# Loads and filler at the start of a gated attention and gMLP kernel: split weight loads, another queue for the gate row, fewer filler matmuls

## Chip, cores and metric

The kernel runs on one core of one Trainium2 chip. The metric is the device time of one execution in microseconds (us); the median of several runs counts.

## What is computed

All arrays are bfloat16. x has 2048 rows of 512. Two mixers read the same x and are blended by a gate per row:

```python
g = sigmoid((x * gate_w).sum(-1, keepdims=True))
# A: linear attention, 32 heads of 16, with a learned feature map
q, k, v = split(x @ wqkv)                  # wqkv is 512 x 1536
phi(t) = concat(softmax(t @ w_phi), softmax(-(t @ w_phi)))
kv = sum_s phi(k)_s v_s ;  z = sum_s phi(k)_s
a = ((phi(q) @ kv) / (phi(q) . z + 1e-6)) @ wo
# B: gMLP, F = 1376, halves of 688
z = gelu(x @ w_in)                         # w_in is 512 x 1376
z1 = z[:, :688] ;  z2 = layernorm(z[:, 688:])
b = (z1 * (w_sp @ z2 + b_sp[:, None])) @ w_out      # w_sp is 2048 x 2048
out = g * a + (1 - g) * b
```

## The kernel before

Rows of x are handled in 16 tiles of 128 (index tt), the inner dimension of 512 in 4 blocks of 128 (index dt). The first stage computes z2 and z1 for all tiles: each tile needs 4 blocks times 2 column halves (j = 0, 1) of 344 columns, one matmul each (z_one, L195), with a transposed tile of x (xT) as weights and a block of w_in as moving data. The second half of w_in (for z2) is in the tile w_z2 and the first half (for z1) in w_z1. w_z2 has one column more, index 688, that holds gate_w, so that the matmul with j = 1 is 345 wide and gives the gate's logit on the side. That column is written by gate_T: gate_w is loaded as 4 rows of 128 (gaterow), transposed by a matmul with an identity (L294), and copied into w_z2 by VectorE (L295).

The order on TensorE and ScalarE is written out by hand (manual_schedule); VectorE and GpSimd are ordered by the tile framework. The head of the order is z2_first_two, which does tiles 0 and 1 together while their data arrive. It holds:

- warm_up(n, w): n filler matmuls of width w on constants, into a bank that is overwritten later (L226);
- x_T(i, d0, d1, ...): transposes of x tile i from the tile xs on TensorE (L284), copied to xT by VectorE (L290) or ScalarE (L287);
- one(tt, dt, j): one z_one matmul for tile tt, block dt, half j.

Then come z2 of tiles 2 and 3, z1 of tiles 0 to 3, and z2 and z1 of tiles 4 to 15 in groups of four, with the folding of w_phi into the query and key weights in between (wphi_fold, fold). After that come keys, values and the spatial product, then queries, attention and the output product.

Loads are issued from three queues, each in program order: SyncE (SP), ScalarE (ACT) and GpSimd (POOL). At the start ACT issues w_z2 blocks 0 and 1, the gate row and w_z2 block 3. SP issues xs tile 0, xs tile 1, w_z2 block 2, xs tiles 2 and 3 in one, then w_z1 in two loads, the transposing loads of x tiles 4 to 15 (L135, L137), w_phi (L140), the transposing load of the query and key weights (wqkT, L141), wv (L142) and the transposing loads of w_sp (wspT, L147). GpSimd issues the row of b_sp (L118) between its memsets. The framework gives the loads of SP and ACT together eight completion counters in turn, so that a load waits until the one eight places before it has landed. In the kernel before the first w_z1 load (L132) is the ninth, and waits for w_z2 block 0.

Of the kernel before, what the change touches and what calls it, by code (L numbers as in the profile page):

```python
# [14 lines left out]
P = 128  # L15
S = 2048
D = 512
H = 32
DH = 16
F = 1376  # L20
FH = 688
HF = FH // 2
NT = S // P
NDT = D // P
# [11 lines left out]
def kernel(  # L36
# [14 lines left out]
    nc = tc.nc  # L51
# [11 lines left out]
    w_z1 = early.tile([P, NDT, FH], BF16, name="w_z1")  # L63
    w_z2 = early.tile([P, NDT, WP], BF16, name="w_z2")
    wv_sb = kvw.tile([P, NDT, D], BF16, name="wv_sb")
# [29 lines left out]
    gaterow = early.tile([P, P], BF16, name="gaterow")  # L95
# [3 lines left out]
    w_in_v = B_w_in.rearrange("(dt p) f -> p dt f", p=P)  # L99
# [7 lines left out]
        out=ramp[:, 0, :], data0=ones32[:, :], data1=zeros[:, :], initial=0.0,  # L107
# [4 lines left out]
    for q in range(4):  # L112
        qs = slice(32 * q, 32 * q + 32)
        nc.vector.tensor_tensor(
            out=ident[qs, qs], in0=ramp[qs, 0, :], in1=ramp[qs, 1, :], op=ALU.is_equal)
    nc.gpsimd.memset(brow[:], 0.0)
    nc.gpsimd.memset(wphiE[:], 0.0)
    nc.gpsimd.dma_start(out=brow[0:NT, :], in_=B_b_sp.rearrange("(t p) -> t p", p=P))  # L118
    def load_z2w(eng, dt):
        eng.dma_start(out=w_z2[:, dt, 0:FH], in_=w_in_v[:, dt, FH:F])  # L120

    nc.sync.dma_start(out=xs[:, 0, :], in_=x2[0:P, :])
    load_z2w(nc.scalar, 0)
    nc.sync.dma_start(out=xs[:, 1, :], in_=x2[P:2 * P, :])
    load_z2w(nc.scalar, 1)
    load_z2w(nc.sync, 2)
    nc.scalar.dma_start(out=gaterow[0:NDT, :], in_=gate_w.rearrange("(dt p) -> dt p", p=P))
    load_z2w(nc.scalar, 3)
    nc.sync.dma_start(
        out=xs[:, 2:4, :], in_=x2[2 * P:4 * P, :].rearrange("(i p) d -> p i d", p=P))  # L130
    for h in range(2):
        nc.sync.dma_start(  # L132
            out=w_z1[:, 2 * h:2 * h + 2, :], in_=w_in_v[:, 2 * h:2 * h + 2, 0:FH])
    for i in range(4, 8):
        nc.sync.dma_start_transpose(out=xT[:, :, i * P:(i + 1) * P], in_=x2[i * P:(i + 1) * P, :])  # L135
    for q in range(2, NCH):
        nc.sync.dma_start_transpose(  # L137
            out=xT[:, :, q * CH:(q + 1) * CH], in_=x2[q * CH:(q + 1) * CH, :]
        )
    nc.sync.dma_start(out=wphiE[0:DH, :, :], in_=A_w_phi.rearrange("h e f -> e h f"))  # L140
    nc.sync.dma_start_transpose(out=wqkT[:, :, :], in_=A_wqkv[:, 0:2 * D])  # L141
    nc.sync.dma_start(  # L142
        out=wv_sb[:, :, :],
        in_=A_wqkv[:, 2 * D:3 * D].rearrange("(dt p) n -> p dt n", p=P),
    )
    for q in range(NCH):
        nc.sync.dma_start_transpose(  # L147
            out=wspT[:, :, q * CH:(q + 1) * CH], in_=B_w_sp[q * CH:(q + 1) * CH, :]
# [4 lines left out]
        out=eexp[:, :], in_=eexp[:, :], pattern=[[0, 8], [-1, 16]],  # L153
# [4 lines left out]
        out=mask_bd[:], in_=mask_bd[:], pattern=[[-16, 8], [0, 16]],  # L158
# [3 lines left out]
        out=mask_bd[:], in_=mask_bd[:], pattern=[[16, 8], [0, 16]],  # L162
# [4 lines left out]
        out=mask4[:], in_=mask4[:], pattern=[[-32, NG]],  # L167
# [3 lines left out]
        out=mask4[:], in_=mask4[:], pattern=[[32, NG]],  # L171
# [3 lines left out]
        out=mask64[:, :, :], in_=mask4[:, :, None].to_broadcast([P, NG, DH]))  # L175
# [7 lines left out]
    def next_turn(kind, n):  # L183
        turn[kind] += 1
        return f"{kind}{(turn[kind] - 1) % n}"

    def zp_tile():
        return psA.tile([P, 2, CH], FP32, name="zp", tag=next_turn("zp", 3))

    def pq_tile(shape, dtype=FP32):  # L190
        return psF.tile(shape, dtype, name="pq", tag=next_turn("pq", 2))

    def z_one(zp, tt, wt, w, dt, j):
        n = HF if j == 0 else w - HF
        nc.tensor.matmul(  # L195
            zp[:, j, 0:n], lhsT=xT[:, dt, tt * P:(tt + 1) * P],
            rhs=wt[:, dt, j * HF:j * HF + n],
            start=(dt == 0), stop=(dt == NDT - 1),
        )
# [8 lines left out]
    def z2_out(tt, zp):  # L208
        z2v = z2all[:, tt, :].rearrange("p (j n) -> p j n", j=2)
        nc.scalar.activation(out=z2v, in_=zp[:, :, 0:HF], func=AF.Gelu_apprx_tanh)  # L210
        nc.vector.tensor_copy(out=glog[:, tt:tt + 1], in_=zp[:, 1, HF:HF + 1])
        for j in range(2):
            nc.vector.bn_stats(out=bn6[:, tt, j, :], in_=z2v[:, j, :])  # L213
        nc.vector.bn_aggr(out=mv[:, tt, :], in_=bn6[:, tt, :, :].rearrange("p j s -> p (j s)"))
# [4 lines left out]
    def z2_first_two():  # L219
        zps = [zp_tile() for _ in range(2)]  # L220
        tp1 = psA.tile([P, 2, P], BF16, name="tp1", tag=next_turn("zp", 3))
        turn["zp"] -= 1

        def warm_up(n, w=CH):
            for _ in range(n):
                nc.tensor.matmul(  # L226
                    zps[0][:, 1, 0:w], lhsT=nc.const_aps.tensor(1.0, [P, P], BF16),
                    rhs=nc.const_aps.tensor(1.0, [P, w], BF16), start=True, stop=True)

        def one(tt, dt, j):  # L230
            z_one(zps[tt], tt, w_z2, FH + 1, dt, j)

        warm_up(6)
        warm_up(5, P)
        x_T(0, 0, 1, pq_tile([P, 1, P], BF16)[:, :, :])
        x_T(0, 1, NDT, pq_tile([P, 3, P], BF16)[:, :, :], on_act=True)
        warm_up(3, P)
        one(0, 0, 0)
        x_T(1, 0, 2, tp1[:, :, :])
        x_T(1, 2, NDT, pq_tile([P, 2, P], BF16)[:, :, :], on_act=True)  # L240
        one(0, 1, 0)
        warm_up(2, P)
        one(1, 0, 0)
        one(1, 1, 0)
        gate_T()
        one(0, 2, 0)
        one(1, 2, 0)
        for dt in range(2):
            one(0, dt, 1)
            one(1, dt, 1)  # L250
        one(0, 2, 1)
        one(1, 2, 1)
        x_T(2, 0, NDT, pq_tile([P, NDT, P], BF16)[:, :, :])
        one(0, 3, 0)
        one(0, 3, 1)
        z2_out(0, zps[0])
        one(1, 3, 0)
        one(1, 3, 1)
        z2_out(1, zps[1])
        x_T(3, 0, NDT, pq_tile([P, NDT, P], BF16)[:, :, :])  # L260
# [21 lines left out]
    def x_T(i, d0, d1, tp, on_act=False):  # L282
        for dt in range(d0, d1):
            nc.tensor.transpose(tp[:, dt - d0, :], xs[:, i, dt * P:(dt + 1) * P], ident[:, :])  # L284
        dst = xT[:, d0:d1, i * P:(i + 1) * P]
        if on_act:
            nc.scalar.copy(out=dst, in_=tp)  # L287
        else:
            with tc.high_priority():
                nc.vector.tensor_copy(out=dst, in_=tp)  # L290

    def gate_T():
        gt = pq_tile([P, NDT])
        nc.tensor.matmul(gt[:, :], lhsT=gaterow[:, :], rhs=ident[:, 0:NDT], start=True, stop=True)  # L294
        nc.vector.tensor_copy(out=w_z2[:, :, FH], in_=gt[:, :])  # L295
# [40 lines left out]
    with tc.manual_schedule(engines={mybir.EngineType.PE, mybir.EngineType.Activation}):  # L336
        z2_first_two()
        z2_tile(2)
        z2_tile(3)
        b_T()  # L340
        for c in range(NCH):
            ts = list(range(c * 4, c * 4 + 4))
            for tt in ts:
                if c > 0:
                    z2_tile(tt)
                if c >= 2 and tt % 4 == 1:
                    later = fold(3 - c)
            for tt in ts:
                z1_tile(tt)
                if c >= 2 and tt % 2 == 0:  # L350
                    later.pop(0)()
            z2_norm(ts)
            if c == 1:
                wphi_fold()
# [264 lines left out]
```

The softmax here doesn't subtract the row's maximum and nothing guards it: scores larger than these inputs give would overflow.

## Time and profile before

| | |
|---|---|
| median of 11 runs | 208.87 us (208.43 to 209.98) |
| profiled execution, its own time | 208.87 us |
| its span, first to last instruction | 207.1 us |
| TensorE matmul busy | 202.3 us, 98% of the span |
| VectorE / ScalarE / GpSimd busy | 128.9 / 77.0 / 46.6 us |
| z matmuls (L195), 256 of them | 39.6 us |
| first filler matmul | at 0.85 us |
| first transpose of x (L284) | at 3.89 us |
| first matmul of z2 tile 2 | at 8.84 us |

All of it is from one profiled execution. PE is TensorE's matmul side and PEld its weight loads, DVE is VectorE; an engine's name with q is its instruction queue, where loads are issued. In lists by instruction the columns are start in us, duration in us, engine, line, operation, what it writes <- what it reads, shape and count; a bracket gives the idle time before it and what ended it. Matmuls overlap, so durations of neighbours are longer than the distance between their starts; the distance is the cost. In a row of a time window the columns are the window, its length, busy time and number of instructions for PE, PEld, DVE, ACT and POOL, the granted TensorE clock, the DMA engines' busy share and GB/s. "Landing" of a load is counted from the start of its issue.

### The profile page before, as it was taken

The numbers are of one execution on the slowest core, as the hardware profiler recorded it, in microseconds if no ns is written. First come the engines' busy times: TensorE is split into PE (matmuls) and PEld (weight loads), VectorE is DVE, ScalarE is ACT, GpSimd is POOL, SyncE is SP. The second block draws the span as 40 slices with busy tenths as digits, with TensorE's granted clock in tenths as the row PEclk, the third lists the DMA queues.
The fourth block names the chain that finished last, engine by engine and source line by source line (L and its number), as shares of the span: only waits on it lengthen the run. The fifth ranks groups of instructions, "written<-read, shape, count | busy, mean of one in ns | idle before, by whom it ended". The sixth has DMA issues, their size and how long they took to land.

```text
span 207.1 us, 3949 instructions
## 1 busy us (share of the span) xinstructions
PE 202.3 (98%) x1534; PEld 121.7 (59%) x1552; DVE 128.9 (62%) x278; ACT 77.0 (37%) x124; POOL 46.6 (22%) x78
## 2 busy tenths in 40 slices
PE   8999999999999999999999999999999999999994
PEld 4666666665566555556565666555455555665642
DVE  2477766665977777879797788555466553633330
ACT  3665668786322232333323032222251126002322
POOL 7020202020542327243342422222204220200000
PEclk9999999999999999999999999999999999999999
DMA  6999999999942015961413229856654567553442
GB/s 187 238 181 228 222 290 218 266 245 239 235 107 40 3 38 99 329 101 28 89 26 66 51 38 111 154 107 67 111 155 65 103 104 189 60 104 68 127 91 78
DMA packets 88971, 27.22 MB, mean 131 GB/s; under 512 B 82968, under 2 KB 88952, under 8 KB 88952
## 3 DMA queue, kind: packets, MB, share of 16 engines
q1 hardware_dynamic: 86176, 24.37, 62.6%
q10 hardware_dynamic: 2744, 2.60, 3.9%
q8 instruction: 12, 0.20, 0.4%
q14 instruction: 7, 0.06, 0.1%
q0 software_dynamic: 32, 0.00, 0.0%
HBM read 4.41 MB, written 2.10 MB: 31 GB/s over the span
## 4 chain that ended last, share of the span: by engine, by line
PE 98%; issue 0%; DVE 0%
PE mm L463 36%; PE zp L195 19%; PE mm L372 13%; PE mm L502 8%; PE mm L412 7%; PE mm L500 7%; PE at L476 2%; PE kvacc L428 2%; PE zp L226 2%; PE mm L505 1%; PE pq L284 1%; PE zp L324 0%; PE pq L324 0%; DVE ob L512 0%; PE pq L305 0%
## 5 line engine op out<-in xcount | busy, mean ns | idle before, releaser
L463 PE MATMUL mm<-z2all,wspT 128*128 128x344 bf16 x512 | 79.9, 309 | 0.0
L463 PEld LDWEIGHTS <-wspT 128*128 128x128 bf16 x512 | 49.0, 98 | 25.7 <-issue 0.4
L195 PE MATMUL zp<-w_z,xT 128*128 128x344 bf16 (+1 forms) x256 | 39.6, 312 | 0.0
L376 ACT ACTIVATE eq<-mm 128x512 bf16<-128x512 f32 x32 | 17.4, 594 | 51.3 <-PE mm L372 21.3
L380 DVE TENSOR_REDUCE zs<-eq 128x64 f32<-128x1024 bf16 x16 | 19.5, 1220 | 20.3 <-ACT eq L376 20.3
L195 PEld LDWEIGHTS <-xT 128*128 128x128 bf16 x256 | 24.8, 99 | 11.9 <-issue 0.2
L468 DVE SCALAR_TENSOR_TENSOR ucat<-mm,bT,z1all 128x344 bf16<-128x344 f32 x32 | 17.4, 544 | 21.9 <-PE mm L463 21.9
L389 POOL TENSOR_TENSOR eq<-eq,ratio 128x512 bf16<-128x512 bf16 x16 | 16.9, 1059 | 50.1 <-DVE ratio L388 41.7
L376 ACT ACTIVATE ek<-mm 128x512 bf16<-128x512 f32 x32 | 17.3, 600 | 27.2 <-PE mm L372 27.2
L516 ACT ACTIVATE ob<-mm,g_inv 128x512 bf16<-128x512 f32 (+1 forms) x16 | 10.9, 681 | 32.8 <-PE mm L505 28.3
L380 DVE TENSOR_REDUCE zs<-ek 128x64 f32<-128x1024 bf16 x16 | 19.3, 1209 | 2.8 <-ACT ek L376 2.8
L502 PE MATMUL mm<-wspT,uT 128*128 128x512 bf16 (+2 forms) x85 | 20.1, 366 | 0.0
L372 PEld LDWEIGHTS <-xT 128*128 128x128 bf16 x128 | 12.2, 98 | 13.0 <-PE mm L505 0.8
L389 POOL TENSOR_TENSOR ek<-ek,ratio 128x512 bf16<-128x512 bf16 x16 | 16.9, 1059 | 2.0 <-DVE ratio L388 1.2
L372 PE MATMUL mm<-wq_p,xT 128*128 128x512 bf16 x55 | 16.0, 379 | 0.5
L412 PE MATMUL mm<-wv_sb,xT 128*128 128x512 bf16 x64 | 16.4, 379 | 0.0
L372 PE MATMUL mm<-wk_p,xT 128*128 128x512 bf16 x61 | 16.2, 379 | 0.2
L500 PE MATMUL mm<-wspT,oT 128*128 128x512 bf16 (+2 forms) x62 | 15.6, 365 | 0.3
L213 DVE BATCH_NORM_STATS2 bn<-z2all 128x6 f32<-128x344 bf16 x32 | 14.9, 502 | 0.0
L210 ACT ACTIVATE z2all<-zp 128x688 bf16<-128x688 f32 x16 | 11.8, 744 | 6.9 <-PE zp L195 6.5
L264 ACT ACTIVATE z1all<-zp 128x688 bf16<-128x688 f32 x16 | 11.9, 744 | 5.1 <-PE zp L195 5.1
L502 PEld LDWEIGHTS <-uT 128*128 128x128 bf16 x85 | 8.2, 98 | 9.2
(80 smaller groups left out, 148.3 us busy)
## 6 DMA issues: line engine op xcount, KB each, us to landing
out_dram<-ob ACTq DMA_DIRECT2D x15, 128.0 KB, 1.8
wspT<-in_B_w_out_dram SPq DMA_DIRECT2D x2, 640.0 KB, 5.0
w_z<-in_B_w_in_dram SPq DMA_DIRECT2D x2, 344.0 KB, 5.4
w_z<-in_B_w_in_dram ACTq DMA_DIRECT2D x3, 172.0 KB, 3.4
wv_sb<-in_A_wqkv_dram SPq DMA_DIRECT2D x1, 512.0 KB, 5.0
wspT<-in_A_wo_dram SPq DMA_DIRECT2D x1, 512.0 KB, 4.8
xs<-in_A_x_dram SPq DMA_DIRECT2D x2, 128.0 KB, 3.0
xs<-in_A_x_dram SPq DMA_DIRECT2D x1, 256.0 KB, 4.8
```

Source lines behind the costliest of these rows:

```text
L195: nc.tensor.matmul(zp[:, j, 0:n], lhsT=xT[:, dt, tt * P:(tt + 1) * P], rhs=wt[:, dt, j * HF:j * HF + n], start=(dt == 0), stop=(dt == NDT ...
L213: nc.vector.bn_stats(out=bn6[:, tt, j, :], in_=z2v[:, j, :])
L264: nc.scalar.activation(out=z1all[:, tt, :].rearrange("p (j n) -> p j n", j=2), in_=zp[:, :, 0:HF], func=AF.Gelu_apprx_tanh,)
L372: nc.tensor.matmul(ps[:, :], lhsT=xT[:, dt, tt * P:(tt + 1) * P], rhs=w[:, dt, :], start=(dt == 0), stop=(dt == NDT - 1))
L376: nc.scalar.activation(out=e[:, :, a, :], in_=ps[:, :].rearrange("p (h f) -> p h f", f=DH), func=AF.Exp, scale=1.0 - 2.0 * a)
L380: nc.vector.tensor_reduce(out=z[:].rearrange("p h a -> p (h a)"), in_=e[:].rearrange("p h a f -> p (h a) f"), axis=AX.X, op=ALU.add,)
L389: nc.gpsimd.tensor_tensor(out=e[:, :, 1, :], in0=e[:, :, 1, :], in1=ratio[:, :, None].to_broadcast([P, H, DH]), op=ALU.mult)
L412: nc.tensor.matmul(v_ps[:, :], lhsT=xT[:, dt, tt * P:(tt + 1) * P], rhs=wv_sb[:, dt, :], start=(dt == 0), stop=(dt == NDT - 1))
L463: nc.tensor.matmul(gp[:, 0:HF], lhsT=wspT[:, st, tt * P:(tt + 1) * P], rhs=z2all[:, st, j * HF:(j + 1) * HF], start=(st == 0), stop=(st == ...
L468: nc.vector.scalar_tensor_tensor(out=ucat[tt % NU][:, c0 + j * HF:c0 + (j + 1) * HF], in0=gp[:, 0:HF], scalar=bT[:, tt:tt + 1], in1=z1all[ ...
L500: nc.tensor.matmul(acc, lhsT=oT[:, g, :], rhs=wo_t[:, g, c0:c1], start=(g == 0), stop=False)
L502: nc.tensor.matmul(acc, lhsT=uT[:, i + ft, :], rhs=w_main[i][:, ft, c0:c1], start=False, stop=False)
```

## The change

The gate row's load moves from ACT to GpSimd, ahead of the load of b_sp. w_z2 block 0 is loaded in two halves of 344 columns, both from ACT. w_z1 is loaded in four pieces instead of two, wv in two instead of one. In z2_first_two the second warm_up has 2 fillers instead of 5; gate_T moves ahead of one(1, 0, 0), and the warm_up there has 1 filler instead of 2; the four matmuls of block 2 now follow the j = 1 matmuls of blocks 0 and 1. The statement for xs tiles 2 and 3 is not touched.

```diff
+    nc.gpsimd.dma_start(out=gaterow[0:NDT, :], in_=gate_w.rearrange("(dt p) -> dt p", p=P))
     nc.gpsimd.memset(brow[:], 0.0)
     nc.gpsimd.memset(wphiE[:], 0.0)
     nc.gpsimd.dma_start(out=brow[0:NT, :], in_=B_b_sp.rearrange("(t p) -> t p", p=P))
...
     nc.sync.dma_start(out=xs[:, 0, :], in_=x2[0:P, :])
-    load_z2w(nc.scalar, 0)
+    nc.scalar.dma_start(out=w_z2[:, 0, 0:HF], in_=w_in_v[:, 0, FH:FH + HF])
     nc.sync.dma_start(out=xs[:, 1, :], in_=x2[P:2 * P, :])
+    nc.scalar.dma_start(out=w_z2[:, 0, HF:FH], in_=w_in_v[:, 0, FH + HF:F])
+    load_z2w(nc.sync, 2)
     load_z2w(nc.scalar, 1)
-    load_z2w(nc.sync, 2)
-    nc.scalar.dma_start(out=gaterow[0:NDT, :], in_=gate_w.rearrange("(dt p) -> dt p", p=P))
     load_z2w(nc.scalar, 3)
     nc.sync.dma_start(
         out=xs[:, 2:4, :], in_=x2[2 * P:4 * P, :].rearrange("(i p) d -> p i d", p=P))
-    for h in range(2):
-        nc.sync.dma_start(
-            out=w_z1[:, 2 * h:2 * h + 2, :], in_=w_in_v[:, 2 * h:2 * h + 2, 0:FH])
+    for dt in range(NDT):
+        nc.sync.dma_start(out=w_z1[:, dt, :], in_=w_in_v[:, dt, 0:FH])
...
-    nc.sync.dma_start(
-        out=wv_sb[:, :, :],
-        in_=A_wqkv[:, 2 * D:3 * D].rearrange("(dt p) n -> p dt n", p=P),
-    )
+    for h in range(2):
+        nc.sync.dma_start(
+            out=wv_sb[:, 2 * h:2 * h + 2, :],
+            in_=A_wqkv[h * 2 * P:(h + 1) * 2 * P, 2 * D:3 * D].rearrange("(dt p) n -> p dt n", p=P),
+        )
...
         warm_up(6)
-        warm_up(5, P)
+        warm_up(2, P)
         x_T(0, 0, 1, pq_tile([P, 1, P], BF16)[:, :, :])
...
         one(0, 1, 0)
-        warm_up(2, P)
+        gate_T()
+        warm_up(1, P)
         one(1, 0, 0)
         one(1, 1, 0)
-        gate_T()
-        one(0, 2, 0)
-        one(1, 2, 0)
         for dt in range(2):
             one(0, dt, 1)
             one(1, dt, 1)
-        one(0, 2, 1)
-        one(1, 2, 1)
+        for j in range(2):
+            one(0, 2, j)
+            one(1, 2, j)
         x_T(2, 0, NDT, pq_tile([P, NDT, P], BF16)[:, :, :])
```

## The prediction

> **What bounds the kernel now.** I read the page first (busy shares, then the chain that ended last), then the chain in order of time, then single instructions of the first 8 us and the landing times of the loads.
>
> ```profile
> PE 202.3 (98%) x1534; PEld 121.7 (59%) x1552; DVE 128.9 (62%) x278; ACT 77.0 (37%) x124; POOL 46.6 (22%) x78
> ...
> PE 98%; issue 0%; DVE 0%
> ```
>
> TensorE (PE) is the chain from end to end: 202.3 of 207.1 us. Loads matter only where PE would wait for one, and the change lies in the first 8 us. There the chain in order of time reads (start, duration, what):
>
> ```profile
> 0.85 3.25 PE zp L226 x11
> 4.10 0.43 PE pq L284 x4
> 4.53 0.32 PE zp L226 x3
> ...
> 6.06 0.57 PE zp L195 x2
> 6.64 1.34 PE zp L195 x8
> 7.97 0.22 PE pq L284 x4
> ```
>
> L226 is filler (warm_up): 16 matmuls on constants whose result nobody reads. Two L195 matmuls take 0.57 us before 6.64, eight take 1.34 after; four transposes (L284) take 0.43 before and 0.22 after. So PE doubles its pace, at about 6.55 us by the single starts (6.14 to 6.42 is a slow one, 6.50 to 6.67 a mixed one, then 0.147 each). The granted-clock column says 1.00 throughout, so it does not show this step; the spacing does. I call this moment the flip.
>
> Single instructions around the two places that the change touches:
>
> ```profile
> 3.78 0.31 PE L226 MATMUL zp<-const-bfloat16-1.0 128*128 128x128 bf16 x1
> 3.81 0.45 PEld L284 LDWEIGHTS <-xs 128*128 128x128 bf16 x4
> 3.89 0.31 PE L284 MATMUL pq<-ident,xs 128*128 128x128 bf16 x1
> ```
>
> ```profile
> 6.42 0.21 PE L294 MATMUL pq<-ident,gaterow 128*128 128x4 bf16 x1
> 6.50 0.34 PE L195 MATMUL zp<-w_z,xT 128*128 128x344 bf16 x1
> 6.70 0.18 DVE L295 CAST w_z<-pq 128x4 bf16<-128x4 f32 x1 [1.03 <-PE pq L294]
> 6.93 0.45 PE L195 MATMUL zp<-w_z,xT 128*128 128x345 bf16 x2
> ```
>
> First: the filler ends exactly where xs tile 0 arrives (issued 0.81, landing 3.0 later, 3.81). Second: the first 345-wide matmul needs the gate column, whose cast ends at 6.88. Its turn was at 6.82 (6.67 + 0.147), so PE lost 0.11 us. That is the only PE wait at the start.
>
> **The change part by part.** PE's list loses four 128-wide fillers: three of five at 3.46 to 3.89, and one of two after one(0,1,0), whose place gate_T takes. In front of the flip one costs 0.107 us.
>
> Front: without the three fillers PE is ready at 3.57 instead of 3.89. It needs xs tile 0. Bounds: lands at 3.81 as now (nothing won) or early enough (0.32 won). The window rows:
>
> ```profile
> 2.00:2.50 0.50, 0.50 (x2) 0.15 (x1) 0.30 (x2) 0.00 (x0) 0.50 (x4) 1.00 0.76 90
> 2.50:3.00 0.50, 0.50 (x3) 0.22 (x2) 0.00 (x0) 0.25 (x1) 0.48 (x3) 1.00 0.95 348
> ```
>
> The last column is GB/s. xs tile 0 (128 KB, SP queue) and w_z2 block 0 (172 KB, ACT queue) leave together and land 0.1 apart (3.81, 3.91), so they share the engines. With 86 KB as the first half beside xs, 88 kB less at 348 GB/s is 0.25 us: xs at 3.56. A waiting transpose starts 0.08 after that (weight load 3.81, matmul 3.89): 3.64, so 0.25 won; I take this, nearer to the better end because the two rows above show the sharing.
>
> The next steps keep their distances: copies of xT end 0.25 earlier too, and one(0,1,0) stands at 5.10. It needs w_z2 block 1, which lands at 4.66 now (1.22 + 3.4). It is issued third instead of second, after two loads of about 0.45, so at 1.7; if the same delay of 0.45 shows at landing, 5.11. No loss, or 0.01; with the 1.0 us that separates the two landings 3.1 and 4.2 on this queue, 0.6 lost. I take none, since the bytes ahead of it are unchanged.
>
> gate_T then stands at 5.39 and costs 0.08 as now (6.42 to 6.50); filler 5.47; one(1,0,0) 5.58; one(1,1,0) 5.86; the first 345-wide one 6.15. The cast needs 0.51 from gate_T (6.42 to 6.93): ready at 5.90. The 0.11 wait is gone, hidden behind two slow matmuls of 0.287; with fast ones (0.147 each) and a fast filler 0.08 of it would remain. After that one(1,0,1) straddles the flip (6.44 to 6.64), six follow at 0.147, and x_T(2) starts at 7.52 against 7.81: **0.29 won**. The same in two terms: 0.25 + 0.107 of slow work saved, of which half counts because the flip is where it was and the rest would have run at twice the pace (0.18), plus 0.11. xs tiles 2 and 3 land at 7.02 and w_z2 block 3 at 6.57, both in time; if xs came 0.5 later than 7.02, the gain would begin to shrink.
>
> The clock rule, weighed by itself: the Trainium skill, "TensorE: Matmul & The Clock Gate", Part 1, says the clock is released after a busy window of about 3.4 us that runs free of the kernel. That fits a flip that stays put, but it speaks against removing filler: a window that no longer counts as busy would cost another 3.4 us at half pace, an estimate of +1.7 from that page.
>
> The flip is known for one execution. Worked the same way, with it at 6.0 the start of x_T(2) goes 7.75 to 7.25 (0.50 won), at 7.0 7.92 to 7.74 (0.18).
>
> Gate row: it leaves the ACT queue (1.76, 0.58 of issue) for GpSimd, ahead of the b_sp row, which holds that slot now:
>
> ```profile
> L118 POOL DMA_DIRECT2D brow<-in_B_b_sp_dram x1: 748/748/748, 1.4 to 1.4; - x1
> ...
> DMA to landing us min/median/max: 3.6/3.6/3.6
> ```
>
> Same slot: issued 1.42, landing 5.02, needed at 5.39 (0.37 in hand). Queued behind it on GpSimd are the b_sp row and the masks, 0.75 later: b_sp lands 5.8 for use at 11.18, the masks end at 5.3 for use at 25.7. Nothing on ACT is later: four loads end near 2.6, now 2.73, and the table load follows.
>
> By "DMA: Bandwidth & Descriptors", Specifications, a load from GpSimd has its first byte at about 1 us against 0.6 on the hardware queues; that would put this row 0.4 later, and the sum would keep its 0.29 if the b_sp row's 3.6 already holds it.
>
> The rest costs nothing in the sum. The order on SP is unchanged: xs 0, xs 1, w_z2 block 2, xs 2 and 3 stand so in both, so that part of the description moves nothing on SP. w_z1 in four adds two issues of 0.42: landing near 10.9 for use at 11.1 to 11.9, later than the 10.0 (4.44 + 5.6) of now; were the last one 1.3 later still, a gap of 0.3 would show at the first z1 tile. SP's later work moves by 0.8, then 1.3 after wv: xT tile 4 lands at 11.6 for use at 16.0, wqkT at 23.1 (15.83 + 6.5 + 0.8) for 27.9, wv near 26.5 for 47.5, the first wspT slab near 35 for 48.4. Cover is over 4 us each.
>
> Sum: 208.87 (this execution's own time, equal to the median of eleven; span 207.1 and 1.77 outside) - 0.29 = **208.58**.
>
> **Rivals.** No transfer gain: xs tile 0 does not come earlier, so the removed filler turns into a wait. Left are 0.107 / 2 + 0.11 = 0.16: 208.7. For it: a 3.0 landing with 0.31 us of bytes at 348 GB/s in front is mostly something else. Against: the two loads landing together.
>
> Gate row late (slower): gate_T is in PE's order, so everything behind it waits. Until 6.55 a late microsecond costs half, after that all. The gain is eaten at a landing of 5.97, and 0.2% is lost from 6.68 (0.58 + 0.13 = 0.71). Loads of that stretch took up to 5.6 (w_z1): at 1.42 + 5.6 = 7.02 the cost is 0.58 + 0.47, the time 209.6. For it: its place moves forward while its queue changes. Against: 3.6 in the same slot, under the same traffic.
>
> Flip elsewhere: each microsecond of shift is half a microsecond. The eleven times spread over 1.55 us, as a flip spread of 3.1 would make them. A later flip with less filler gives 209.4 at 1.7 later; one 1 us earlier in the runs of after, or the 6.0 case above, 208.1 to 208.4.
>
> **How the numbers follow.** 0.2% (0.42 us) is about what a measurement of this kernel can tell from no change. Forecast 0.60, its own range 208.35 to 208.75: with 0.18, 0.29 and 0.50 as gains and the spread of the runs, 0.28 of it counts beyond 0.42 and 0.32 within. No transfer gain 0.08, within. Earlier flip 0.12, faster. Gate row late 0.12 and later flip 0.08, slower. Faster 0.40, same 0.40, slower 0.20. The range 208.0 to 209.2 takes in the w_z1 gap of 0.3, the 0.6 at block 1 and both no-gain cases, and leaves out most of the slower fifth.
>
> **What would show it.** Right: the first L284 near 3.64, gate_T near 5.4 with no idle, the first 345-wide matmul with no wait for L295, x_T(2) near 7.5, the rest at the old distances. Wrong: PE idle before L284 until 3.8, idle before L294 with the GpSimd load as releaser, a wait at one(0,1,0), a gap at the first z1 tile, or slow L195 matmuls after 6.6.

## The result and the profile after

The changed kernel takes 211.09 us (median of 13 runs, 209.14 to 212.39) against 208.66 us beside it (median of 50): slower, with a ratio of 1.0084, 95% interval 1.0065 to 1.0104. The ratios here leave out single disturbed runs, so they are not quite the ratio of the medians. The thirteen times fall into two groups, five from 209.14 to 209.77 and eight from 211.07 up; the experiments explain both the step from 208.7 to 209.4 and the step from there to 211.2. The profiled execution is of the upper group: 211.6 us, span 209.9.

The page after, busy shares and the chain that ended last:

```profile
PE 202.6 (97%) x1530; PEld 121.2 (58%) x1548; DVE 129.0 (61%) x278; ACT 77.0 (37%) x124; POOL 47.0 (22%) x79
...
PE 95%; DMA 3%; issue 1%; ACTq 0%; DVE 0%
```

PE is as busy as before (202.6 for 202.3), but the chain now holds 3% of a load. The waits of PE name it (us in total, times, longest):

```profile
PE zp L196 <- DMA w_z<-in_B_w_in_dram: 2.6, 1, 2.6
PE zp L227 <- PEq L603: 0.8, 1, 0.8
```

The second line is the kernel's start, as before. The first is new: one wait of 2.6 us. The instructions show where (line numbers have moved by one: L196 is z_one, L227 the filler):

```profile
3.60 0.34 PEld L284 LDWEIGHTS <-xs 128*128 128x128 bf16 x4
3.61 0.53 PE L284 MATMUL pq<-ident,xs 128*128 128x128 bf16 x4
...
4.48 0.28 PE L284 MATMUL pq<-ident,xs 128*128 128x128 bf16 x2
...
7.37 0.44 PE L196 MATMUL zp<-w_z,xT 128*128 128x344 bf16 x1 [2.62 <-DMA w_z<-in_B_w_in_dram]
7.61 0.21 PE L294 MATMUL pq<-ident,gaterow 128*128 128x4 bf16 x1
```

The transposes start at 3.61 instead of 3.89. The matmul at 7.37 is one(0,1,0), which needs w_z2 block 1. Block 1 was issued at 1.71 and landed 5.6 later; before it was issued at 1.24 and landed 3.4 later. The same matmul before, and the first matmul of z2 tile 2 before and, in the second block, after:

```profile
5.35 0.49 PE L195 MATMUL zp<-w_z,xT 128*128 128x344 bf16 x1
...
8.84 2.50 PE L195 MATMUL zp<-w_z,xT 128*128 128x344 bf16 x16
```

```profile
11.72 2.50 PE L196 MATMUL zp<-w_z,xT 128*128 128x344 bf16 x16
```

What the wait does to TensorE stands in the window rows (the third column from the right is the granted clock):

```profile
5.00:6.00 1.00, 0.00 (x0) 0.00 (x0) 0.00 (x0) 0.98 (x2) 0.14 (x1) 1.00 1.03 342
6.00:7.00 1.00, 0.00 (x0) 0.00 (x0) 0.00 (x0) 0.47 (x1) 0.00 (x0) 1.00 1.07 382
7.00:8.00 1.00, 0.63 (x4) 0.39 (x4) 0.11 (x1) 0.00 (x0) 0.00 (x0) 0.67 0.90 326
8.00:9.00 1.00, 1.00 (x5) 0.56 (x4) 0.06 (x1) 0.00 (x0) 0.00 (x0) 0.50 0.27 77
9.00:10.00 1.00, 1.00 (x5) 0.50 (x4) 0.00 (x0) 0.00 (x0) 0.00 (x0) 0.50 1.09 102
10.00:11.00 1.00, 1.00 (x8) 0.68 (x7) 0.00 (x0) 0.00 (x0) 0.00 (x0) 0.62 0.79 138
11.00:12.00 1.00, 1.00 (x12) 0.72 (x10) 0.50 (x2) 0.59 (x1) 0.00 (x0) 1.00 0.48 112
```

Idle in 5 to 7, then half the clock from about 7.3 to 10.8, then full. The books close: one(0,1,0) could start 0.60 earlier than before (4.75 for 5.35, half of it from the front and half from an earlier step to full pace in this execution); the wait puts it 2.02 later (7.37 for 5.35); from there to the first matmul of z2 tile 2 it takes 4.35 instead of 3.49. That is the half clock: 3.4 of the 4.35 were at half pace, against 1.2 of the 3.49 (up to the step at about 6.55). That matmul starts at 11.72 for 8.84, 2.88 later, and the spans differ by 2.8.

The bytes are not missing. The ACT queue (q10), packets, MB and share of 16 engines, in the windows 4 to 5, 5 to 6, 6 to 7 and 7 to 8 us, one line each:

```profile
q10 hardware_dynamic: 118, 0.14, 64.8%
...
q10 hardware_dynamic: 97, 0.11, 31.9%
...
q10 hardware_dynamic: 8, 0.01, 2.3%
...
q10 hardware_dynamic: 8, 0.01, 2.6%
```

Of 576 packets all but 16 had started by 6.0, and these 16 belong to blocks 1 and 3. The trace records the completion of each load in sixteen parts. Fifteen parts of block 1 were complete between 4.68 and 5.29, the last one at 7.33, and that is when PE went on. Before the change all sixteen came between 4.30 and 4.65.

### The profile page after: what moved, and what is told of

Read it like the earlier page. It is cut to its first block, busy times and chain, and to the rows that moved or that the text cites. A ratio compares the mean times of both kernels' runs of the same rounds, so it can differ in the third digit from the quotient of the medians.

```text
span 209.9 us, 3946 instructions
## 1 busy us (share of the span) xinstructions
PE 202.6 (97%) x1530; PEld 121.2 (58%) x1548; DVE 129.0 (61%) x278; ACT 77.0 (37%) x124; POOL 47.0 (22%) x79
## 4 chain that ended last, share of the span: by engine, by line
PE 95%; DMA 3%; issue 1%; ACTq 0%; DVE 0%
PE mm L463 36%; PE zp L196 19%; PE mm L372 13%; PE mm L502 8%; PE mm L412 7%; PE mm L500 6%; DMA w_z<-in_B_w_in_dram 3%; PE at L476 2%; PE kvacc L428 2%; PE mm L505 1%; PE zp L324 0%; PE pq L284 0%; ACTq L126 0%; ACTq L124 0%; PE pq L324 0%
## 5 line engine op out<-in xcount | busy, mean ns | idle before, releaser
L196 PE MATMUL zp<-w_z,xT 128*128 128x344 bf16 (+1 forms) x256 | 40.3, 317 | 2.6 <-DMA w_z<-in_B_w_in_dram 2.6
L196 PEld LDWEIGHTS <-xT 128*128 128x128 bf16 x256 | 25.1, 100 | 12.6
```

What stands on the lines that cost most here:

```text
L196: nc.tensor.matmul(zp[:, j, 0:n], lhsT=xT[:, dt, tt * P:(tt + 1) * P], rhs=wt[:, dt, j * HF:j * HF + n], start=(dt == 0), stop=(dt == NDT ...
```

## The experiments

Four explanations were open: the gate row's software load, the split of block 0 (which makes block 1 the third load on ACT), w_z1 in four loads, and TensorE's new order. "From after" and "from before" say which kernel was edited.

**The gate row back on ACT**, from after:

```diff
-    nc.gpsimd.dma_start(out=gaterow[0:NDT, :], in_=gate_w...)
+    nc.scalar.dma_start(out=gaterow[0:NDT, :], in_=gate_w...)      # between blocks 1 and 3
```

> The changed kernel with the gate row back on ACT's queue, between w_z2 blocks 1 and 3; all else as changed. Software-queue theory (two loads from GpSimd instead of one hold up one of the 16 DMA engines, so that w_z2 blocks 1 to 3 land 2.5 us late): block 1 lands near 4.7 to 5.0, no long wait at one(0,1,0), 208.3 to 208.7. Split theory (block 0 in halves puts block 1 third on ACT): the wait of 2.6 us stays, near 211. w_z1 theory (four loads issued from 3.4 compete): the wait stays, near 211.

209.57 us, 1.0062 (1.0037 to 1.0086), three of ten times near 211. A wait of 1.2 us at one(0,1,0) until 6.47. The software load is not the main cause.

**Block 0 whole**, from after:

```diff
-    nc.scalar.dma_start(out=w_z2[:, 0, 0:HF], ...)
-    nc.scalar.dma_start(out=w_z2[:, 0, HF:FH], ...)
+    load_z2w(nc.scalar, 0)
```

> The changed kernel with w_z2 block 0 in one load again, so that block 1 is second on ACT; one load less means that the first w_z1 load no longer waits for a counter and is issued near 2.7. Software-queue theory: the wait for block 1 stays in most runs, 210 to 211. Split theory: block 1 lands near 4.7 as before the change, 208.4 to 208.8. w_z1 theory: w_z1 starts even earlier, so the wait is as long or longer, 211 or more.

208.67 us, 1.0003 (0.9986 to 1.0021). No wait for block 1 in the profile; one of the ten times is 211.17, with a mean granted clock of 0.992, and no trace shows what it waited for. What is left are these two (waits of PE):

```profile
PE pq L293 <- DMA gaterow<-in_gate_w_dram: 0.8, 1, 0.8
...
PE pq L283 <- DMA xs<-in_A_x_dram: 0.2, 1, 0.2
```

So the split carries nearly all of the loss. Behind it stood a second one: the gate row, landing 4.8 after its issue at 1.42, was late for its new place.

**w_z1 in two**, from after:

```diff
-    for dt in range(NDT):
-        nc.sync.dma_start(out=w_z1[:, dt, :], in_=w_in_v[:, dt, 0:FH])
+    for h in range(2): ...      # as before
```

> The changed kernel with w_z1 in two loads as before the change. w_z1 theory: block 1 lands before 5.2 and the time is 208.4 to 208.8. Software-queue and split theories: the wait of about 2.6 us stays, 210 to 211.

211.00 us, 1.0097 (1.0064 to 1.0130); five of eight times above 210.9; one(0,1,0) waits 1.7 until 6.97. w_z1 in four is not the cause.

**TensorE's old order and filler**, from after:

```diff
-        warm_up(2, P)
+        warm_up(5, P)
...
-        gate_T()
-        warm_up(1, P)
+        warm_up(2, P)
...      # gate_T and block 2 where they were before the change
```

> All loads as changed, but TensorE's order and filler as before the change (five and two narrow fillers, gate_T after one(1,1,0), block 2 ahead of the j = 1 matmuls). If the loads themselves land late (any of the three load theories): one(0,1,0) still waits until about 7.3, 2.0 to 2.3 us instead of 2.6 as TensorE comes 0.3 later, 210.5 to 211.5. If the loss comes from TensorE's shorter head reaching data that were always late: back at 208.7 to 209.0.

209.51 us, 1.0059 (1.0034 to 1.0084), two of ten times above 211; one(0,1,0) waits 1.1 until 6.59. The wait was shorter than I expected, but it is there with the old order: the loads are late, TensorE is not early.

**The split alone**, from before:

```diff
-    load_z2w(nc.scalar, 0)
+    nc.scalar.dma_start(out=w_z2[:, 0, 0:HF], ...)
+    nc.scalar.dma_start(out=w_z2[:, 0, HF:FH], ...)
```

> The kernel before with one edit: w_z2 block 0 in two halves, so that block 1 is third on ACT (the gate row fourth, block 3 fifth). Place theory: block 1 lands near 6.4 to 6.8, one(0,1,0) waits 1.0 to 1.5 us; less than 1.5 us of gain from filler that costs nothing, so 209.3 to 209.8, a few runs near 211. If the loss needs the other edits too: 208.5 to 208.9.

209.63 us, 1.0051 (1.0030 to 1.0071):

```profile
6.66 0.31 PE L196 MATMUL zp<-w_z,xT 128*128 128x344 bf16 x1 [1.59 <-DMA w_z<-in_B_w_in_dram]
```

The split alone makes the wait and the step to 209.6. No time was near 211 in six, so the second step is not shown for it. Here too it is one part of block 1 that is late: fifteen were complete by 5.40, the last at 6.62.

**Block 1 second though block 0 is split**, from after:

```diff
+    load_z2w(nc.scalar, 1)
     nc.scalar.dma_start(out=w_z2[:, 0, HF:FH], ...)
-    load_z2w(nc.scalar, 1)
```

> The changed kernel with ACT's order block 0 first half, block 1, block 0 second half, block 3, so that block 1 is second on ACT though block 0 is still split. Place theory (the third load on ACT lands near 6.5 to 7.3 whatever it is, the second near 4.3 to 4.7): no wait at one(0,1,0); instead the first 345-wide matmul, which needs the second half of block 0 from about 5.9, waits 0.5 to 1.3 us, or gate_T waits for its row; 208.6 to 209.6. Size theory (short rows of 688 bytes make everything behind them slow): block 1 stays late, near 211.

208.95 us, 1.0028 (1.0005 to 1.0050). one(0,1,0) runs at 5.03 without a wait; now the gate row is late by 1.4, and the half load of 86 KB that went third, issued at 1.73, lands 5.1 later. So the short rows of the first half do not make the load behind them late.

**No software load at the start**, from after:

```diff
-    nc.gpsimd.dma_start(out=gaterow[0:NDT, :], in_=gate_w...)
+    nc.scalar.dma_start(out=gaterow[0:NDT, :], in_=gate_w...)      # between blocks 1 and 3
-    nc.gpsimd.dma_start(out=brow[0:NT, :], in_=B_b_sp...)
+    nc.sync.dma_start(out=brow[0:NT, :], in_=B_b_sp...)            # behind w_z1
```

> The changed kernel with no load from GpSimd at the start: gate row on ACT between blocks 1 and 3, b_sp row on SP behind w_z1; block 0 still split, block 1 third on ACT. If a software load holds up one DMA engine: block 1 lands near 5.0, 208.3 to 208.7. If the place alone does it: block 1 lands near 6.4 as with only the gate row moved back, 209.3 to 209.8.

210.02 us (five runs, from 209.09 to 211.05), 1.0077 (1.0044 to 1.0110). Block 1 lands 4.9 after its issue at 1.71, and one(0,1,0) waits 1.76. No software load is needed for the lateness.

**Filler in the wait**, from after:

```diff
+        warm_up(8)
         one(0, 1, 0)
```

> The changed kernel with 8 more wide fillers ahead of one(0,1,0), 1.7 us of work at full pace, so that TensorE is busy during most of the wait for block 1. Clock theory (the idle wait of 2.6 us makes the clock fall to half for a window of 3.4 us, which costs the upper times near 211 about 1.7 us more than the lower near 209.3): no time above 210.3, median 209.2 to 209.8, and no window with a granted clock of 0.5 after the first full one. If the upper times come from a later landing instead: still half of them near 211.

> The same kernel as fill_wait, for more times. Clock theory: none above 210.3. Landing theory: about half near 211, as with the changed kernel.

209.59 us (four runs, 1.0067, 1.0045 to 1.0088) and 209.36 us (six runs, 1.0041, 1.0025 to 1.0056). None of the ten times is above 209.99, against eight of thirteen above 211 without it. Eight matmuls that compute nothing make the kernel 1.5 and 1.7 us faster at the median. The window rows of the first show a full clock where the changed kernel had 0.50:

```profile
7.00:8.00 1.00, 1.00 (x8) 0.56 (x7) 0.18 (x1) 0.00 (x0) 0.00 (x0) 1.00 1.07 390
8.00:9.00 1.00, 1.00 (x8) 0.68 (x7) 0.00 (x0) 0.00 (x0) 0.00 (x0) 1.00 1.03 249
```

So the upper group is the clock: near 209.4 with the wait alone, near 211.2 when the wait also halves the clock. The recorded mean clock agrees as far as it goes: 0.990 to 0.992 in four of the eight upper times and in the profiled one, and never under 0.997 in a time below 210.3 of any kernel here. The other four upper times are recorded with 1.00. That does not rule a drop out, as the column said 1.00 before the step at 6.55 too, at half pace; for these four the filler runs are the evidence.

**The other parts alone.** TensorE's new head on the loads of before:

```diff
-        warm_up(5, P)
+        warm_up(2, P)
...      # and the new order from one(0, 1, 0) to x_T(2)
```

> The kernel before with TensorE's new head alone (four fillers fewer, gate_T earlier, block 2 behind the j = 1 matmuls); all loads as before. Place theory: block 1 lands near 4.7 as before, nothing waits but the first transpose (up to 0.25 us for xs tile 0); the 0.11 us at the gate column and the fillers are won: 208.3 to 208.6, 0.1 to 0.4 under the kernel before beside it. If the shorter head itself costs (a later clock, a new wait): 208.8 or more.

208.48 us, 0.9998 (0.9983 to 1.0013): no wait at all, the first transpose at 3.75. The median is 0.13 under the kernel beside it, but the interval holds a ratio of 1, so no gain is shown. The gate row on GpSimd alone, from before:

```diff
+    nc.gpsimd.dma_start(out=gaterow[0:NDT, :], in_=gate_w...)      # ahead of the b_sp row
-    nc.scalar.dma_start(out=gaterow[0:NDT, :], in_=gate_w...)
```

> The kernel before with the gate row on GpSimd as the only edit. TensorE needs the row at 6.42 there. With the row landing at 5.6 to 6.7, as in the runs so far, gate_T waits 0 to 0.4 us: 208.6 to 209.0, the same as before. If the software load disturbs the other loads: block 1 lands later than 4.9 and the time is 209.2 or more.

208.97 us, 1.0016 (0.9999 to 1.0033): the row lands 4.6 after its issue, near 6.0. In its profile PE waits 0.3 for a block of w_z2 instead. If anything it costs a little.

**Block 0 whole and the gate row on ACT**, from after:

```diff
-    nc.scalar.dma_start(out=w_z2[:, 0, 0:HF], ...)
-    nc.scalar.dma_start(out=w_z2[:, 0, HF:FH], ...)
+    load_z2w(nc.scalar, 0)
-    nc.gpsimd.dma_start(out=gaterow[0:NDT, :], in_=gate_w...)
+    nc.scalar.dma_start(out=gaterow[0:NDT, :], in_=gate_w...)      # between blocks 1 and 3
```

> Block 0 whole and the gate row back on ACT, with TensorE's shorter head, w_z1 in four and wv in two as changed. Place theory: no wait for block 1 (4.7) and no wait for the gate row (0.85 us with it on GpSimd and block 0 whole); only up to 0.3 us for xs tile 0; the predicted gain of 0.1 to 0.4 shows, 208.2 to 208.6. If w_z1 in four or TensorE's order costs by itself: 208.8 or more.

> The same kernel as best (block 0 whole, gate row on ACT, the rest as changed), with more rounds. 208.2 to 208.5, and a ratio under 1 by 0.1 to 0.2%. If w_z1 in four and wv in two cost nothing, within 0.1 us of the run with TensorE's head alone.

208.25 us, 0.9994 (0.9978 to 1.0010), and in a second set 208.27 us, 0.9979 (0.9965 to 0.9994). It is faster than the changed kernel; than the kernel before by 0.2% in the second set, while the interval of the first set holds a ratio of 1. No wait for a load in either profile. w_z1 in four and wv in two cost nothing that shows; wv was not run by itself.

**What makes block 1 late.** Place on the queue, bytes and rows ahead, issue time, or the traffic of w_z1 were still open. Three kernels, from after:

```diff
 late_w_z1: all SP loads behind xs tiles 2 and 3 wait for six tiny VectorE
            writes into their destinations, made from xT tile 1
 gate_second: block 0 whole; ACT issues block 0, gate row (1 KB), block 1, block 3
 block1_late: block 0 whole; a ScalarE copy into blocks 1 and 3 precedes their loads
```

> The changed kernel with all of SP's loads behind xs tiles 2 and 3 held back until the first copy of xT tile 1 (near 5.0 instead of 3.4), by six small VectorE writes into their destinations; block 0 split, block 1 third on ACT. Traffic theory (w_z1 on SP's queue, issued from 3.4, takes the engines from block 1): block 1 lands by 5.4, 208.4 to 208.9. Place theory: it still lands at 6.4 to 7.3, 209.2 to 211.

> Block 0 whole, then the 1 KB gate row second and block 1 third on ACT, issued near 1.85; the bytes ahead of block 1 are those of before but 1 KB, and no short rows of w_in are left. Place theory: block 1 lands at 6.0 to 7.3, 209.0 to 209.8, some near 211. Bytes or short rows: it lands by 5.2, 208.3 to 208.7.

> Block 0 whole, block 1 second on ACT, but issued near 2.7 instead of 1.2, behind a ScalarE copy into its destination that brings the table load forward. Place theory (a queue's second load lands 3.0 to 3.4 after its issue): 5.7 to 6.1, a wait near 0.8 us, partly hidden by the gate row's: 208.7 to 209.2. Time theory (what is issued after about 1.7 lands late because everything ahead on both queues must pass): 6.5 or later, 209.3 to 211.

Measured: 209.33 us (1.0050, 1.0029 to 1.0070), 210.77 us (1.0086, 1.0058 to 1.0113) and 211.19 us (1.0113, 1.0086 to 1.0139). In this order, one(0,1,0) in the three profiles:

```profile
6.45 0.31 PE L204 MATMUL zp<-w_z,xT 128*128 128x344 bf16 x1 [1.65 <-DMA w_z<-in_B_w_in_dram]
```

```profile
6.75 0.31 PE L195 MATMUL zp<-w_z,xT 128*128 128x344 bf16 x1 [1.65 <-DMA w_z<-in_B_w_in_dram]
```

```profile
7.07 0.38 PE L196 MATMUL zp<-w_z,xT 128*128 128x344 bf16 x1 [2.25 <-DMA w_z<-in_B_w_in_dram]
```

With w_z1 not issued before 5.25 block 1 still lands at 6.4: the traffic of w_z1 falls. With only 1 KB more ahead of it on its queue and no short rows, issued at 1.85, it lands 4.9 later: bytes and rows ahead on ACT fall. As second load, but issued at 2.77, it lands 4.3 later, at 7.07: the place theory falls too. The time theory is left: what is issued from about 1.7 on lands late. It does not tell the time itself from the loads of both queues that are under way by then. Block 1 by issue time:

| kernel | on ACT | issued | landing after |
|---|---|---|---|
| before, pe_only, best, best_again, block0_whole, gate_pool_only | 2nd | 1.2 | 3.1 to 3.5 |
| block1_second | 2nd | 1.24 | 3.0 |
| after | 3rd | 1.71 | 5.6 |
| split_only, no_software, late_w_z1, gate_on_act, old_pe_order | 3rd | 1.7 | 4.7 to 4.9 |
| wz1_in_two, fill_wait, fill_again | 3rd | 1.7 | 4.6 to 5.2 |
| gate_second | 3rd | 1.85 | 4.9 |
| block1_late | 2nd | 2.77 | 4.3 |

Before the change the loads issued from 1.7 on took 4.2 and more as well (w_z2 blocks 2 and 3 4.2, xs tiles 2 and 3 4.8); nothing needed them earlier. Why a load of this second wave takes one or two microseconds more is not settled: the DMA engines are busy in both, and no run here takes all of that away. The parts show what kind of lateness it is. In the changed kernel and in split_only a single part of sixteen comes 1.2 to 2 us after the others. In gate_on_act, late_w_z1 and no_software half the parts of block 1 were complete by 5.1, 4.8 and 5.3 too, and several trail until 6.4 to 6.6. In block1_late, issued a microsecond later, all of them come between 6.18 and 7.03, 3.4 to 4.3 after the issue.

## Why the prediction was wrong

**The step that failed** is block 1's landing. The prediction had "issued third instead of second, after two loads of about 0.45, so at 1.7; if the same delay of 0.45 shows at landing, 5.11. No loss, or 0.01". The issue was right (1.71). The landing was 7.33, and 6.3 to 7.0 in the other kernels in which block 1 is third. The bound of 0.6, from "the 1.0 us that separates the two landings 3.1 and 4.2 on this queue", was the right neighbour wrongly used: I took the better end "since the bytes ahead of it are unchanged", while the rows said that both 172 KB loads issued from 1.7 on, blocks 2 and 3, had taken 4.2. 1.71 + 4.2 = 5.9 from the same profile would have meant a wait of 0.8 and a forecast of no gain. In the changed kernel's profile fifteen of the sixteen parts did come about when the prediction said, by 5.29; what it had no term for is the last one, 2.0 later. The loads behind show the same miss: block 3 was put at 6.57 and landed at 8.17, xs tiles 2 and 3 at 7.02 and landed at 8.56, both hidden by the wait for block 1.

**The clock** was named and then left at a page's price. The +1.7 for one lost window was an estimate from the window of about 3.4 us in the Trainium skill, "TensorE: Matmul & The Clock Gate", Part 1. The runs agree with that price, with 0.50 granted from 7.3 to 10.8 and 1.8 us between the means of the two groups (209.43 and 211.21, the latter without the single time of 212.39). The prediction tied that loss to removed filler. It was the load wait that tripped it, and 0.67 in the row 7 to 8 shows the moment. The removed filler alone (TensorE's new head on the loads of before) cost nothing that shows. Nor does the flip stay put, as the sum had it: the trace's clock record begins at 6.60 in the kernel before (the spacing gave 6.55) and at 3.93 in the changed one.

**The gate row** was the slower rival, and it was real, only hidden: predicted to land at 5.02, 3.6 after its issue, it took 3.6 to 5.3 in the kernels that load it from GpSimd, 4.2 in the changed one, and landed at 5.0 to 6.7. It cost waits of 0.8 and 1.4 us in two kernels in which block 1 was in time. "Same slot" was a weak reason: one landing of 3.6 said little about the spread in that slot.

**What held**: the front. xs tile 0 was put at 3.56 and the first transpose at 3.64; it starts at 3.61. Of the shorter head's gain the kernel with block 0 whole and the gate row on ACT shows a sign at most: 208.27 against 208.61, a ratio of 0.9979. There xs tile 0 comes no earlier (transposes at 3.89), and for that case the prediction had 0.16; the medians differ by 0.13 with the head alone, within the noise, and by 0.34 here. That w_z1 and wv would cost nothing was right as far as the runs tell.

## What to carry to other kernels

Splitting a load to bring its first half forward delays whatever stands behind it on that queue by one issue; here, at the start of the kernel, half a microsecond of issue became 1.7 to 2.7 of landing. So read the landing times of all loads of the same stretch by their issue time before moving one, and take the row of the neighbours that it will be among after the move. Where TensorE may have to wait for a load early on, try filler in front of the wait: here it cost nothing that shows while the load was late, and none of ten times fell into the upper group.

## What the runs showed of the hardware

A wait much shorter than 3.4 us can be followed by half the clock. With no software load the wait is 1.76 us, and yet:

```profile
6.62 0.31 PE L196 MATMUL zp<-w_z,xT 128*128 128x344 bf16 x1 [1.76 <-DMA w_z<-in_B_w_in_dram]
```

```profile
6.00:7.00 1.00, 0.38 (x5) 0.28 (x5) 0.00 (x1) 1.00 (x1) 0.00 (x0) 1.00 0.97 353
7.00:8.00 1.00, 1.00 (x7) 0.53 (x5) 0.17 (x1) 0.21 (x1) 0.00 (x0) 0.67 0.99 352
8.00:9.00 1.00, 1.00 (x5) 0.56 (x4) 0.00 (x0) 0.00 (x0) 0.00 (x0) 0.50 0.72 248
```

PE is at work again from 6.62, and the clock still drops past 7.3 and stays at half until near 10.8. The clock record of this trace runs in stretches of 3.41 us, full from 3.93 to 7.34 and half to 10.76, and the whole wait lies in the first. The table of states in the Trainium skill, "TensorE: Matmul & The Clock Gate", Part 1, has the drop after an idle window of about 3.4 us; here about half a window's idle time was enough, so the measurement decides. The waits of 2.6 us in the changed kernel and 2.25 in block1_late were followed by half the clock as well. Waits of 1.59 (split_only) and 1.65 (late_w_z1, gate_second) kept it full, and they too lie within one stretch, counted on from where their records begin. So in these six profiles the border lies between 1.65 and 1.76 us of wait. A wait of 1.71 in the kernel with w_z1 in two also cost no clock (209.73 us), but its trace has no clock record. What splits the times of one kernel into two groups, a longer wait or its place against the stretches, is not shown: each set of runs has one profile.
